# Block-sparse attention with a feed-forward network: a planner that takes VectorE and GpSimd as excluding each other instruction by instruction, and changes its order by steps of moved turns and backward passes

## The chip, the cores and the metric

The kernel runs on one core of one Trainium2 chip. The metric is the device time in microseconds (us) of one execution; the time before is the median of three runs. The engines are TensorE (PE, with its weight loads as PEld), VectorE (DVE), ScalarE (ACT), GpSimd (POOL) and SyncE (SP), which issues most of the DMAs.

## What is computed

Attention over 4 batches, 8 heads, 768 positions and 64 features a head, in blocks of 32. A block of queries sees its neighbours, the first and the last block, and three sampled blocks; the first and last block see all. What comes out, as 3072 tokens of 512 features, goes through two matrix products with a leaky maximum between them.

```python
# block = 32, n_blocks = 24, sampled_blocks [24, 3]
scores = scale * np.matmul(q, k.transpose(0, 1, 3, 2))
mask = np.abs(blk_i - blk_j) <= 1
mask = mask | (blk_i == 0) | (blk_j == 0) | (blk_i == n_blocks - 1) | (blk_j == n_blocks - 1)
for qb in range(n_blocks):
    for kb in sampled_blocks[qb]:
        mask[qb * block:(qb + 1) * block, kb * block:(kb + 1) * block] = True
scores = np.where(mask, scores, -1000000000.0)
scores = scores - np.max(scores, axis=-1, keepdims=True)
attn = np.exp(scores)
attn = attn / (np.sum(attn, axis=-1, keepdims=True) + 1e-09)
attn_out = np.matmul(attn, v).astype(np.float32)
x = attn_out.transpose(0, 2, 1, 3).reshape(B * S, H * D)      # [3072, 512]
h = x @ w_in                                                  # [512, 2048]
g = np.maximum(0.01 * h, h)
out = (g @ w_out).astype(np.float32)                          # [2048, 512]
```

## The kernel before, in words

**Numbers as pairs.** Every fp32 operand of a large product is scaled and split into a high and a low float16 part, and a product is taken as high x high, high x low and low x high. The low part comes from a subtraction on DVE or POOL.

**Tiles and items.** A tile is 64 queries of one batch with all heads; four tiles make an item of 256 tokens, and there are 12 items. The first tile of a batch, T = 0, holds the queries of the first and the last block and takes all keys. Every other tile takes 256 keys, of which the sampled ones are gathered: the keys kg by POOL copies on the chip (`gather_k`, L1273, the copies at L1295, three of one task), the values vg by an indirect DMA that POOL issues (`gather_v`, L1313, L1328) from scr, where the split values v lie in DRAM. em is a tile's row of the mask.

**One unit of attention** (a tile and a pair of heads) runs through: scores in PSUM, s<-kg,qs and s<-kg,qxs (`unit_scores`, L1357); p<-s,em,nsc on DVE with the extremum mx (`unit_ttr`, L1381); the exponential p<-p,mx on ACT; pp<-p,r on ACT, the high part; pp<-p,r,pp on DVE, the low part (`unit_split`, L1423); the transpose pt, early ones by PE and ACT (o<-eye,pp and pt<-o), later ones by DMA; av<-pt,vg on PE (`pair_av`, L1452). `tile_evac` (L1472) makes the input of the feed-forward network (FFN): avt<-av on ACT, xf<-av,avt on DVE, the high part x<-xf on ACT, the low part x<-xf,x on POOL.

**The FFN.** For each item 16 half blocks of h (`ffn_h`, L1494; 12 products of 128 x 256 each) and as many output blocks o<-W,g (`ffn_o`, L1525), with ht and g in between on ACT, DVE and POOL (`ffn_max` L1512, `ffn_act2` L1517). The first two items take the weights by quarters, as soon as each is there.

**The weights** lie in DRAM as pairs of 32-bit words. `decode` (L965) puts one piece together by one ACT and three DVE instructions (W<-W, and W<-kt,W where the raw words lie in the kt buffer). The squares W<-W on PE, which stand under s<-W in the trace, give ssw; s<-ssw,ones adds it over the partitions; DVE takes the exponent exw from it and from that the scale wi_i, wi_s (or wo_i, wo_s). `finish` (L1030) then splits: W<-W,wi_s on ACT for the high part, and for the low part DVE (W<-W,wo_s), or PE with the diagonal dg and ACT (W<-h). In the same way q gets sc_i, sc_s and qa from ssq and exq.

**The order.** Nothing is issued as it is written. Each operation is recorded as a task with its engine, an estimated duration, what it reads and writes (`Engine`, L602, which is why nearly all rows of the trace have this line). `Plan.order` (L549) then lists them: `trial` (L365) runs a model of the five engines and of the DMA rings forward, where each engine that is free takes the ready task with the lowest priority number (PE adds 400 for a change of array shape); `backward` (L503) goes through the tasks from the end and gives each its latest turn, and these turns are the next trial's priorities. 24 such passes are made, and the best is kept. Then a table of 318 steps, SHIFTS (L194), each an engine, a stretch in units of 100 ns of the model's time, and an amount, is added to the priorities, all by the starts of that one best trial, and one trial gives the order. `issue` (L569) emits it; each engine runs its queue in order.

**The model's port.** DVE and POOL share a way to the on-chip memory. In `take` (L428) a task with the mark `port` starts later by 0.6 of what the other engine's marked task has left:

```python
elif k.port:
    other = "POOL" if e == "DVE" else "DVE"
    at0 += COST["port"] * max(0.0, port[other] - at0)
    port[e] = at0 + busy
```

The functions that the diff touches, with the lines of the profile:

Of the kernel before, what the change touches and what calls it, by code (L numbers as in the profile page):

```python
# [79 lines left out]
    "passes": 24,  # L80
}
# [70 lines left out]
class Task:  # L152
# [3 lines left out]
    def __init__(self, eng, kind="", port=False):  # L156
        self.eng, self.run, self.busy, self.enter, self.kind, self.loads = eng, [], 0.0, kind, kind, []
        self.port, self.parts = port, {}
# [13 lines left out]
class Part:  # L172
# [17 lines left out]
    "port": 0.6,  # L190
# [4 lines left out]
    ("all", 382, 161, 1500), ("PE", 2050, 164, 1500), ("all", 2692, 51, -500), ("all", 308, 13, 1500),  # L195
    ("all", 326, 16, -1500), ("all", 351, 11, -1500), ("all", 2467, 105, -120), ("POOL", 2435, 1, -60),
    ("PE", 1021, 26, -900), ("all", 4744, 25, -1500), ("ACT", 5485, 132, 500), ("all", 5117, 179, -900),
    ("POOL", 2682, 33, 60), ("all", 24, 13, -250), ("PE", 1505, 151, 250), ("all", 7260, 3, -60),
    ("all", 142, 140, -500), ("all", 39, 12, 250), ("SP", 7141, 187, -250), ("all", 1837, 133, 500),
    ("POOL", 3367, 133, -500), ("all", 658, 3, 1500), ("DVE", 2456, 14, 500), ("POOL", 2148, 21, -120),  # L200
    ("DVE", 5777, 39, 1500), ("ACT", 6401, 93, 250), ("DVE", 3285, 33, 1500), ("PE", 6464, 9, 500),
    ("SP", 323, 3, -250), ("PE", 3661, 1, -1500), ("DVE", 4302, 4, 900), ("DVE", 1935, 8, 60),
    ("all", 1583, 68, 900), ("PE", 6984, 1, 60), ("PE", 6019, 8, -900), ("POOL", 1568, 31, 250),
    ("all", 6226, 9, 120), ("ACT", 4881, 11, 30), ("ACT", 1320, 77, -500), ("POOL", 4117, 101, -500),
    ("all", 3109, 18, -900), ("all", 5687, 67, 30), ("all", 4594, 11, 500), ("POOL", 3842, 107, 1500),
    ("SP", 5240, 134, 120), ("ACT", 410, 8, 900), ("all", 7070, 103, 1500), ("ACT", 1074, 34, 500),
    ("PE", 5379, 90, 120), ("POOL", 2446, 35, 500), ("PE", 3340, 6, -60), ("all", 6477, 194, 60),
    ("ACT", 293, 41, -500), ("SP", 48, 89, 250), ("PE", 6718, 1, 30), ("DVE", 6388, 17, 60),
    ("all", 438, 10, -120), ("ACT", 2931, 15, 1500), ("ACT", 3436, 10, -1500), ("SP", 3767, 84, -1500),
# [88 lines left out]
class Plan:  # L298
# [250 lines left out]
    def order(self):  # L549
# [15 lines left out]
        if VERBOSE:  # L565
            print("model", max(best[2]))
# [1422 lines left out]
```

## Time and profile before

| | us |
|---|---|
| median of 3 runs | 742.38 (739.17 to 743.46) |
| profiled execution | 740.85 |
| its span | 739.0 |
| mean granted clock of PE | 0.965 |

| engine | busy, us | share of the span |
|---|---|---|
| PE | 687.2 | 93% |
| DVE | 538.1 | 73% |
| ACT | 466.6 | 63% |
| POOL | 371.2 | 50% |

A row of the timeline has the start, the duration, engine, line, operation, what is written <- what is read, and in brackets how long the engine had been idle before it and which work ended that. The granted clock is a share of full speed: 1.00 is 2.4 GHz, 0.50 is 1.2 GHz. Matmuls of a kind are gathered in one row with their count. The FFN's first product starts at 98.22 us; the work before it is attention for the first item and the first weights.

### The profile page before, as it was taken

What the parts mean: (1) busy time and instruction counts of PE and PEld (TensorE: products, weight loads), DVE (VectorE), ACT (ScalarE), POOL (GpSimd) and SP (SyncE); (2) the same over time, 40 slices, a digit from 0 to 9 for tenths busy, and PEclk for the clock granted to TensorE, in tenths of its full rate; (3) what the DMA queues carried; (4) which work ended last, traced back from release to release, by engine and by line L of the source; (5) the groups of instructions that cost most, each with busy time, mean ns of one, the idle gap of its engine ahead of it and who ended that gap; (6) DMA issues with size and microseconds to landing.
All of it is one profiled execution on the core that took longest, in us unless ns stands there. A gap on an engine that the chain in (4) does not pass through costs nothing.

```text
span 739.0 us, 21165 instructions
## 1 busy us (share of the span) xinstructions
PE 687.2 (93%) x7880; PEld 464.5 (63%) x7880; DVE 538.1 (73%) x1544; ACT 466.6 (63%) x1111; POOL 371.2 (50%) x626
## 2 busy tenths in 40 slices
PE   2675599999999999999999999999999999999997
PEld 2353465656566667667676677666666766767664
DVE  4897998899996878777788658679786766752221
ACT  6987889966964766576667556676584655541211
POOL 1466564556425566565454647546435656632221
PEclk9766699999999999999999999999999999999999
DMA  9739699997999799999998988969995865750100
GB/s 201 257 86 266 212 279 232 227 226 141 178 182 205 151 193 200 185 181 176 196 187 160 201 175 172 198 165 201 169 173 97 173 142 93 150 127 9 44 1 29
DMA packets 261939, 122.63 MB, mean 166 GB/s; under 512 B 230220, under 2 KB 242636, under 8 KB 261836
## 3 DMA queue, kind: packets, MB, share of 16 engines
q1 hardware_dynamic: 254796, 98.20, 68.0%
q0 software_dynamic: 7040, 23.07, 12.2%
q8 instruction: 62, 1.02, 0.6%
q14 instruction: 41, 0.34, 0.2%
HBM read 65.65 MB, written 12.58 MB: 106 GB/s over the span
## 4 chain that ended last, share of the span: by engine, by line
PE 74%; DVE 6%; ACT 6%; issue 3%; DMA 3%; POOL 3%; SPq 0%; POOLq 0%; ACTq 0%; DVEq 0%
PE h L602 32%; PE o L602 31%; PE av L602 6%; PE s L602 5%; DVE W L602 2%; ACT W L602 2%; DMA vg<-scr,vrow 1%; ACT pp L602 1%; DMA pt<-pp 1%; ACT p L602 1%; DMA kt<-in_moe_w_in_dram 1%; DVE p L602 1%; DVE pp L602 1%; POOL allow L602 1%; POOL kg L1295 0%
## 5 line engine op out<-in xcount | busy, mean ns | idle before, releaser
L602 PEld LDWEIGHTS <-W 128*128 128x128 f16 (+1 forms) x2480 | 235.8, 99 | 56.1 <-DVE W L602 7.1
L602 PE MATMUL h<-x,W 128*128 128x256 f16 x2304 | 270.5, 273 | 0.2 <-POOL x L602 0.2
L602 PE MATMUL o<-W,g 128*128 128x512 f16 x1152 | 267.7, 379 | 0.7 <-DVE ob L602 0.6
L602 POOL TENSOR_TENSOR g<-ht,g 128x512 f16<-128x512 f32 x96 | 116.9, 1217 | 175.8 <-DVE g L602 145.4
L602 PEld LDWEIGHTS <-g 128*128 128x128 f16 x1152 | 109.5, 98 | 118.6 <-issue 4.9
L602 DVE SCALAR_TENSOR_TENSOR pp<-p,r,pp 128x256 f16<-128x256 f32 (+1 forms) x208 | 123.5, 612 | 26.5 <-ACT pp L602 25.8
L602 ACT ACTIVATE p<-p,mx 128x256 f32<-128x256 f32 (+1 forms) x208 | 107.1, 516 | 56.2 <-DVE mx L602 53.5
L602 ACT ACTIVATE pp<-p,r 128x256 f16<-128x256 f32 (+1 forms) x208 | 100.3, 515 | 33.3 <-DMA pt<-pp 18.2
L602 ACT ACTIVATE ht<-h,gs 128x512 f32<-128x512 f32 x80 | 54.5, 682 | 102.8 <-PE h L602 81.0
L602 DVE SCALAR_TENSOR_TENSOR ht<-h,gd,ht 128x512 f32<-128x512 f32 x80 | 59.8, 747 | 75.4 <-ACT ht L602 75.1
L1328 POOL DMA_INDIRECT vg<-scr,vrow x88 | 90.8, 1032 | 46.1 <-PE av L602 21.5
L1295 POOL COPY kg<-kt 128x128 int32 x264 | 85.4, 359 | 37.4 <-PE h L602 23.7
L602 DVE CUSTOM_DVE_ANT_0 p<-s,em,nsc 128x256 f32<-128x256 f32 x116 | 52.9, 474 | 14.3 <-PE s L602 13.3
L602 PE MATMUL av<-pt,vg 128*64 128x64 f16 (+1 forms) x2112 | 54.1, 208 | 4.9 <-DMA vg<-scr,vrow 2.5
L602 PEld LDWEIGHTS <-vg 128*64 128x64 f16 x2112 | 45.5, 114 | 19.5 <-issue 16.4
L602 POOL TENSOR_TENSOR x<-xf,x 128x256 f16<-128x256 f32 x48 | 36.1, 753 | 37.2 <-ACT x L602 30.6
L602 DVE CAST g<-ht 128x512 f16<-128x512 f32 x80 | 34.3, 429 | 9.5 <-PE o L602 7.3
L602 PEld LDWEIGHTS <-qs 128*32 128x32 f16 (+1 forms) x768 | 23.5, 98 | 26.2 <-issue 22.5
L602 ACT ACTIVATION_READ_ACCUMULATOR p<-p,mx 128x1 f32 x208 | 39.1, 188 | 0.0
L602 DVE COPY kg<-kt 128x512 f16<-128x512 f16 x96 | 33.8, 365 | 1.5 <-PE h L602 1.5
L602 PE MATMUL s<-kg,qs 128*32 128x256 f16 x464 | 31.4, 287 | 3.1 <-DVE mx L602 2.9
L602 PE MATMUL s<-kg,qxs 128*32 128x256 f16 x464 | 31.0, 283 | 0.0
(129 smaller groups left out, 801.4 us busy)
## 6 DMA issues: line engine op xcount, KB each, us to landing
v<-in_v_dram SPq DMA_DIRECT2D x32, 192.0 KB
qxs<-qs SPq DMA_DIRECT2D x48, 128.0 KB
scr<-v SPq DMA_DIRECT2D x16, 384.0 KB
vg<-scr SPq DMA_DIRECT2D x44, 128.0 KB
rq<-in_q_dram SPq DMA_DIRECT2D x20, 256.0 KB
W<-in_moe_w_in_dram SPq DMA_DIRECT2D x5, 1024.0 KB
out_dram<-ob SPq DMA_DIRECT2D x20, 256.0 KB
rk<-in_k_dram SPq DMA_DIRECT2D x24, 192.0 KB
```

The lines of the kernel that those rows point to most:

```text
L602: self.plan.task(self.eng, lambda: f(*a, **k), busy, late, reads, writes, kind, loads, port)
L1295: tc.nc.gpsimd.tensor_copy(out=kg.ap.bitcast(I32)[:, :, slot * BLOCK // 2:(slot + 1) * BLOCK // 2], in_=kt.ap.bitcast(I32)[:, :, bass.ds(o ...
L1328: tc.nc.gpsimd.indirect_dma_start(into.ap, None, scr[b].ap, bass.IndirectOffsetOnAxis(ap=at.ap, axis=0))
```

## The change

Three things change in the planner; the recorded operations are the same.

1. The model of the port. A port now holds when the other engine's marked task began to use it, a grain, and when it ends. A marked task waits for the whole rest of the other's, DVE's wait less 150 ns. For POOL's task of three copies kg<-kt the wait goes only to the end of the copy that is running (grain 330 ns).
2. SHIFTS is a new table with a fifth field. Each step adds its amount by the starts of the present best trial. With -1 nothing follows; otherwise a trial follows, and then so many backward passes, each with a trial, so that the next step sees new starts and new priorities.
3. Two settings, `xlo` and `glo`, could give the low parts of x and g of the first items to DVE. Both are 0.

```diff
-    "port": 0.6,
+    "port": 150.0,
 SHIFTS = (
-    ("all", 382, 161, 1500), ("PE", 2050, 164, 1500), ("all", 2692, 51, -500), ("all", 308, 13, 1500),
...
+    ("all", 716, 15, 500, -1), ("all", 192, 105, -60, 0), ("all", 130, 4, -30, 0), ("SP", 650, 128, 500, 0),
+    ("PE", 2232, 131, 60, -1), ("all", 1454, 144, 60, -1), ("all", 1428, 110, 250, 0),
...
-        mode, port = [""], {"DVE": 0.0, "POOL": 0.0}
+        mode, port = [""], {"DVE": (0.0, 0.0, 0.0), "POOL": (0.0, 0.0, 0.0)}
...
             elif k.port:
-                other = "POOL" if e == "DVE" else "DVE"
-                at0 += COST["port"] * max(0.0, port[other] - at0)
-                port[e] = at0 + busy
+                since, grain, until = port["POOL" if e == "DVE" else "DVE"]
+                rest = until - at0 if at0 >= since else 0.0
+                if rest > 0 and grain:
+                    rest = min(rest, grain - (at0 - since) % grain)
+                at0 += max(0.0, rest - (COST["port"] if e == "DVE" else 0.0))
+                port[e] = at0 + k.port[0], k.port[1], at0 + busy
...
-        if SHIFTS:
-            for eng, at, wide, by in SHIFTS:
-                for i, k in enumerate(self.tasks):
-                    if eng in ("all", k.eng) and at * 100.0 <= best[1][i] < (at + wide) * 100.0:
-                        prio[i] += by
+        for eng, at, wide, by, passes in SHIFTS:
+            for i, k in enumerate(self.tasks):
+                if eng in ("all", k.eng) and at * 100.0 <= best[1][i] < (at + wide) * 100.0:
+                    prio[i] += by
+            if passes < 0:
+                continue
             best = self.trial(prio, CFG["stay"])
+            for _ in range(passes):
+                prio = self.backward(best[1], best[2])
+                best = self.trial(prio, CFG["stay"])
...
             plan.task("POOL", copies, t, t, cells(kt) | cells(offs),
-                      cells(kg[:, :, at:at + NR * BLOCK]) | {("registers",)}, port=True)
+                      cells(kg[:, :, at:at + NR * BLOCK]) | {("registers",)},
+                      port=(t - CFG["kcopy"] * NR, CFG["kcopy"]))
...
-        nc.gpsimd.tensor_tensor(out=xs[:, 1], in0=xf, in1=xs[:, 0], op=ALU.subtract)
+        (nc.vector if it.n < CFG["xlo"] else nc.gpsimd).tensor_tensor(out=xs[:, 1], in0=xf, in1=xs[:, 0], op=ALU.subtract)
```

The order moves nearly everywhere. Three places follow. In the rows a name's number is that of its buffer, so av0 and s1 are PSUM banks, and W_84 is the whole weight store.

**PE, near 67 us of the trace of before.** First before, where the sum s1_64<-ssw1_180 stands behind four groups of products with vg0_88:

```order
L602 MATMUL av0_70<-pt4_155,vg0_88 64x2x32
...
L602 MATMUL av0_70<-pt3_149,vg0_88 64x128
L602 LDWEIGHTS ones_74
L602 MATMUL s1_64<-ssw1_180,ones_74 128x1
L602 LDWEIGHTS qs1_168
L602 MATMUL s1_64<-kg0_86,qs1_168 32x256
```

Then with the change:

```order
L576 MATMUL s1_64<-kg0_86,qxs1_169 32x256
L576 LDWEIGHTS ones_74
L576 MATMUL s1_64<-ssq2_170,ones_74 128x1
L576 LDWEIGHTS ones_74
L576 MATMUL s1_64<-ssw1_180,ones_74 128x1
L576 LDWEIGHTS pp3_143
L576 MATMUL o1_66<-eye16_76,pp3_143 128x128
...
L576 LDWEIGHTS vg0_88
L576 MATMUL av0_70<-pt2_148,vg0_88 64x2x32
```

The sum of squares of a weight piece has moved ahead of the first product with the gathered values, and the sum for the third half of q stands beside it.

**DVE, around the xf of the fourth tile of the first item (91.92 us in the trace of before).** Before:

```order
L602 SCALAR_TENSOR_TENSOR xf_179<-av0_70,avt_177 128x256
L602 TENSOR_SCALAR W_84<-W_84 128x1024
L602 TENSOR_SCALAR wi1_i_189<-exw2_188 128x1
L602 SCALAR_TENSOR_TENSOR W_84<-kt0_85,W_84 128x1024
L602 RECIPROCAL wi1_s_190<-wi1_i_189 128x1
L602 SCALAR_TENSOR_TENSOR W_84<-W_84 128x1024
L602 ISA p0_114,mx4_157<-s0_63,em1_165,nsc5_193 128x256
L602 ISA mx4_157 128x1
L602 ISA p1_115,mx5_159<-s1_64,em1_165,nsc5_193 128x256
L602 ISA mx5_159 128x1
L602 SCALAR_TENSOR_TENSOR xf_179<-av0_70,avt_177 128x256
L602 SCALAR_TENSOR_TENSOR W_84<-W_84 128x1024
```

With the change; the first row is that xf:

```order
L576 SCALAR_TENSOR_TENSOR xf_179<-av0_70,avt_177 128x256
L576 RECIPROCAL wi1_s_190<-wi1_i_189 128x1
L576 RECIPROCAL sc_s3_126<-sc_i3_125 128x1
L576 SCALAR_TENSOR_TENSOR W_84<-W_84,wo0_s_183 128x2x512
L576 TENSOR_SCALAR W_84<-W_84 128x1024
L576 ISA p0_114,mx4_157<-s0_63,em1_165,nsc5_193 128x256
L576 ISA mx4_157 128x1
L576 SCALAR_TENSOR_TENSOR W_84<-kt0_85,W_84 128x1024
L576 ISA p1_115,mx5_159<-s1_64,em1_165,nsc5_193 128x256
L576 ISA mx5_159 128x1
```

The two p, the scales wi_s and sc_s, one split W<-W,wo_s and one decoding step W<-kt,W stood ahead of the fourth xf and now stand behind it.

**PE, around the h block at 165.9 us of the trace of before.** Before, two score blocks stand ahead of h0_67:

```order
L602 MATMUL o1_66<-W_84,g1_211 128x512
L602 LDWEIGHTS qs0_102
L602 MATMUL s1_64<-kg0_86,qs0_102 32x256
...
L602 LDWEIGHTS qs0_102
L602 MATMUL s0_63<-kg0_86,qs0_102 32x256
...
L602 LDWEIGHTS W_84
L602 MATMUL h0_67<-x1_212,W_84 128x256
...
L602 MATMUL s0_63<-W_84 128x128
```

With the change:

```order
L576 MATMUL s1_64<-kg0_86,qxs0_103 32x256
L576 LDWEIGHTS W_84
L576 MATMUL h0_67<-x1_212,W_84 128x256
...
L576 MATMUL s0_63<-W_84 128x128
...
L576 MATMUL s1_64<-ssw3_195,ones_74 128x1
L576 LDWEIGHTS W_84
L576 MATMUL h1_68<-x1_212,W_84 128x256
...
L576 LDWEIGHTS qs0_102
L576 MATMUL s0_63<-kg0_86,qs0_102 32x256
```

The second of the two score blocks, s0_63<-kg0_86,qs0_102, has moved behind the squares of W and four half blocks of h.

## Rows read from the trace of the kernel before

**Rows 1.** The page: busy time of each engine, and the chain that ended last.

```profile
PE 687.2 (93%) x7880; PEld 464.5 (63%) x7880; DVE 538.1 (73%) x1544; ACT 466.6 (63%) x1111; POOL 371.2 (50%) x626
PE 74%; DVE 6%; ACT 6%; issue 3%; DMA 3%; POOL 3%; SPq 0%; POOLq 0%; ACTq 0%; DVEq 0%
```

**Rows 2.** Stretches: us, busy of PE, PEld, DVE, ACT, POOL, PEclk, DMA share, GB/s.

```profile
0.00:62.00 62.00, 32.80 (x365) 23.71 (x365) 46.75 (x138) 50.91 (x102) 27.42 (x71) 0.81 0.66 183
62.00:85.90 23.90, 13.63 (x178) 10.36 (x179) 19.81 (x52) 18.72 (x39) 14.40 (x23) 0.50 0.96 285
85.90:98.20 12.30, 8.47 (x106) 4.43 (x106) 11.25 (x30) 8.87 (x20) 7.14 (x12) 0.86 0.67 200
98.20:165.00 66.80, 65.47 (x695) 40.74 (x694) 61.37 (x158) 58.81 (x129) 35.96 (x56) 1.00 1.11 234
165.00:200.00 35.00, 33.90 (x379) 22.00 (x379) 32.67 (x99) 27.50 (x67) 19.40 (x35) 1.00 0.84 160
200.00:260.00 60.00, 58.87 (x689) 39.27 (x687) 48.83 (x142) 39.50 (x96) 27.47 (x49) 1.00 0.95 181
260.00:700.00 440.00, 439.56 (x5252) 302.45 (x5251) 309.58 (x921) 256.76 (x657) 231.37 (x374) 1.00 0.83 158
700.00:739.00 39.00, 34.52 (x223) 21.52 (x220) 7.82 (x14) 5.50 (x8) 8.08 (x7) 0.98 0.04 14
```

**Rows 3.** Timeline near 69 us: start, duration, engine, line, operation, idle time before.

```profile
59.37 1.32 POOL L1328 DMA_INDIRECT vg<-scr,vrow  x1 [0.30 <-issue]
...
67.09 1.82 PE L602 MATMUL av<-pt,vg 128*64 128x64 f16 x44 [2.49 <-DMA vg<-scr,vrow]
...
68.84 0.18 PE L602 MATMUL s<-ssw,ones 128*128 128x1 bf16 x1
68.95 0.38 ACT L602 ACTIVATE avt<-av 128x256 f32<-128x256 f32 x1 [2.15 <-PE av L602]
...
69.63 0.16 DVE L602 TENSOR_SCALAR exw<-s 128x1 int32<-128x1 int32 x1 [3.18 <-PE s L602]
```

**Rows 4.** Timeline of DVE, 83.9 to 92.3 us.

```profile
83.93 0.15 DVE L602 RECIPROCAL sc_s<-sc_i 128x1 f32<-128x1 f32 x1
...
84.39 1.27 DVE L602 SCALAR_TENSOR_TENSOR W<-W,wo_s 128x1024 f16<-128x1024 f32 x1
...
88.12 1.70 DVE L602 SCALAR_TENSOR_TENSOR W<-kt,W 128x1024 int32<-128x1024 int32 x1
...
91.34 0.47 DVE L602 CUSTOM_DVE_ANT_0 p<-s,em,nsc 128x256 f32<-128x256 f32 x1
...
91.92 0.42 DVE L602 SCALAR_TENSOR_TENSOR xf<-av,avt 128x256 f32<-128x256 f32 x1
92.26 1.22 DVE L602 SCALAR_TENSOR_TENSOR W<-W 128x1024 int32<-128x1024 int32 x1
```

**Rows 5.** Timeline of ACT, 84.6 to 93.3 us.

```profile
84.61 0.71 ACT L602 ACTIVATE qa<-rq,sc_s 128x512 f16<-128x512 f32 x1
...
89.93 1.15 ACT L602 ACTIVATE W<-W,wi_s 128x1024 f16<-128x1024 f32 x1 [1.94 <-DVE wi_s L602]
...
93.24 0.58 ACT L602 ACTIVATE W<-h 128x512 f16<-128x512 f32 x1
```

**Rows 6.** Timeline: the FFN's first product, and PE's wait at 165.5 us.

```profile
95.20 0.66 POOL L602 TENSOR_TENSOR x<-xf,x 128x256 f16<-128x256 f32 x1
...
98.22 1.47 PE L602 MATMUL h<-x,W 128*128 128x256 f16 x12
...
165.52 0.29 PE L602 MATMUL s<-kg,qs 128*32 128x256 f16 x4 [1.61 <-DVE mx L602]
```

**Rows 7.** Timeline at 281 us; then one group of DVE, 165 to 200 us.

```profile
280.73 2.67 DVE L602 SCALAR_TENSOR_TENSOR pp<-p,r,pp 128x256 f16<-128x256 f32 x1 [0.34 <-ACT pp L602]
281.43 0.75 POOL L1295 COPY kg<-kt 128x128 int32 x3
...
L602 DVE SCALAR_TENSOR_TENSOR pp<-p,r,pp 128x256 f16<-128x256 f32 x11 | 8.4, 760 | 0.2 <-ACT pp L602 0.2
```

More of the change, by code (lines that the diff above doesn't have):

```diff
@@ L80 @@
     "passes": 24,
+    "xlo": 0,
+    "glo": 0,
 }
@@ L200 @@
[L200 to L209, printed above, removed]
@@ new lines @@
+    ("SP", 944, 70, 900, -1), ("SP", 6232, 109, 3000, -1), ("POOL", 1093, 1, -500, 0),
+    ("all", 1328, 52, 500, -1), ("SP", 1866, 5, -900, -1), ("POOL", 4575, 186, -3000, 0),
+    ("DVE", 994, 113, 900, -1), ("all", 3191, 16, 500, 0), ("PE", 717, 5, -900, -1), ("all", 326, 32, -500, -1),
+    ("all", 6756, 190, 500, 0), ("all", 1599, 37, -60, -1), ("DVE", 4960, 24, 1500, -1),
+    ("POOL", 430, 29, -120, 0), ("POOL", 1340, 154, -500, -1), ("SP", 1885, 8, 60, -1),
+    ("ACT", 6214, 105, -60, 0), ("SP", 195, 5, 60, -1), ("all", 4628, 9, -500, 0), ("all", 91, 44, -250, 0),
@@ new lines @@
+    ("all", 930, 144, -1500, 0), ("all", 4086, 8, 900, 0), ("all", 1994, 31, -120, -1),
+    ("PE", 6386, 13, -1500, -1), ("SP", 1636, 31, 3000, 0), ("PE", 4055, 7, 900, -1),
+    ("POOL", 1824, 5, -250, -1), ("SP", 6793, 12, -30, 0), ("all", 1254, 26, 60, -1), ("ACT", 252, 3, 900, -1),
+    ("DVE", 1009, 16, -250, 0), ("all", 5292, 8, -1500, 0), ("PE", 5617, 15, -1500, -1),
+    ("ACT", 7273, 3, -900, -1), ("ACT", 5987, 22, -30, 0), ("SP", 1127, 3, 500, 0), ("all", 323, 124, 900, -1),
+    ("all", 6658, 5, 1500, 0), ("PE", 1414, 86, -250, -1), ("ACT", 5300, 116, 250, 0),
@@ new lines @@
+    ("ACT", 776, 165, 900, 0), ("all", 307, 18, 120, -1), ("all", 5165, 38, 3000, 0), ("SP", 108, 3, -60, -1),
+    ("all", 446, 7, -250, 0), ("DVE", 4136, 3, -250, -1), ("all", 591, 9, 120, 0), ("all", 144, 2, -120, 0),
+    ("SP", 1685, 23, 3000, 0), ("POOL", 325, 7, 3000, -1), ("POOL", 1357, 6, 120, -1), ("all", 968, 3, 900, 0),
+    ("DVE", 7286, 21, 250, -1), ("SP", 6796, 8, -30, -1), ("all", 1433, 152, -500, 0), ("SP", 327, 4, 1500, 0),
+    ("all", 318, 1, 250, 0), ("POOL", 1087, 2, -120, -1), ("POOL", 909, 29, -30, 0), ("SP", 781, 4, 60, -1),
@@ new lines @@
+    ("all", 5462, 29, 120, 0), ("all", 1971, 23, 1500, 0), ("all", 1432, 26, -500, 0),
+    ("POOL", 1120, 105, -30, 0), ("ACT", 492, 22, -900, 0), ("DVE", 377, 32, -3000, 0),
+    ("POOL", 1183, 174, 30, 0), ("POOL", 1032, 4, 500, -1), ("ACT", 59, 22, 900, 0), ("ACT", 228, 12, 120, -1),
+    ("all", 1315, 3, -3000, 0), ("PE", 108, 69, 3000, 0), ("PE", 88, 1, -1500, 0), ("SP", 2706, 23, 500, 0),
+    ("all", 248, 15, -1500, -1), ("PE", 181, 31, -900, -1), ("SP", 3057, 1, 3000, 0), ("PE", 424, 2, 900, -1),
@@ L270 @@
+    ("all", 5084, 2, 120, 0), ("ACT", 5170, 3, 30, 0), ("all", 6149, 34, -30, 0), ("PE", 2621, 2, 60, -1),
+    ("POOL", 1176, 25, 120, 0), ("ACT", 5662, 45, -1500, 0), ("POOL", 1506, 51, -250, -1),
[3 rows of a table added]
 )
@@ L307, in __init__, with task @@
             setattr(self, name, Engine(self, name, eng))
-    def task(self, eng, run, busy, late, reads, writes, kind="", loads=(), port=False):
+    def task(self, eng, run, busy, late, reads, writes, kind="", loads=(), port=None):
         if self.group is not None and eng == self.group.eng:
```

76 lines of the change are left out of this document (12 added, 64 removed), and 9 rows, old and new, of the table SHIFTS.

## The prediction

> **What bounds the kernel now.** I read the page's busy times first, then the chain that ended last, then busy time stage by stage, and last the timelines at the places where TensorE (PE) waits. PE is busy 93% of the span and holds 74% of the chain [rows 1]; no other engine comes near over the whole run. An average hides the stages, so the table by stretch decides [rows 2]. From 260 to 700 us PE is busy 439.56 of 440.00: nothing but less PE work, or fewer waits than 0.44, can help there, and both orders hold the same instructions. From 98.2 to 260 PE loses 1.33, 1.10 and 1.13 us in three stretches. From 700 it loses 4.48 of 39.00. What is left lies ahead of 98.2 us, where the feed-forward network (FFN) starts: PE works 32.80 of the first 62 us, then 13.63 of 23.90 at a granted clock of 0.50, then 8.47 of 12.30 at 0.86. There VectorE (DVE) is the fullest engine: 19.81 of 23.90 and 11.25 of 12.30. A start that is one us shorter there is worth one us of the run, as long as what DVE and ScalarE (ACT) put off does not hold PE up behind it. That condition is a hard one: DVE is still busy 61.37 of 66.80 and 32.67 of 35.00 in the next two stretches, so it has 5.43 and 2.33 us free [rows 2].
>
> **The port rule by itself.** It changes what the planner believes, not an instruction. No row of time belongs to it; it can act only through the order. The two new settings are 0 and move nothing. So the price is that of the new order, and I go by its places.
>
> **The stall at 69 us.** In the trace of before the gather of v into vg was issued at 59.37, and PE waited 2.49 us for it before the 44 products av<-pt,vg at 67.09 [rows 3]. Behind those on PE stands one matmul of 0.18 us, s<-ssw,ones at 68.84, the sum of squares from which a weight quarter gets its scale. DVE waited 3.18 us for it before exw<-s at 69.63, and ACT waited 2.15 us for the same 44 products before avt<-av [rows 3]. This is the dearest single stall of DVE ahead of the FFN. In the new order that matmul stands ahead of the first product with vg, with only score blocks ahead of it whose data are there. If the gather lands as late as before, PE still waits, but DVE and ACT go on with the scale, the split and the decoding of weights. What is late next is DVE's own queue of decoding. The row says 3.18 us of DVE come free, and bounds are 0 (DVE only finds another wait) and -3.2; I take **-3.2**, since DVE is at 19.81 of 23.90 there and the difference, 4.09, is little more than this one stall. ACT's own stall there lies beside it and is not counted again.
>
> **Work put off behind the start of the FFN.** The first product h<-x,W runs at 98.22; its last input is the low part of x from GpSimd (POOL) at 95.20, 0.66 us long [rows 6], which follows xf<-av,avt of the fourth tile on DVE at 91.92 [rows 4]. In the new order eight instructions that stood ahead of that xf on DVE come behind it: the first is sc_s (0.15, at 83.93), the dearest are W<-W,wo_s (1.27) and W<-kt,W (1.70), the last is the second p<-s,em,nsc (0.47, at 91.34) [rows 4]. Together they take 5.63 us; one W<-W of 1.22 comes ahead instead [rows 4], so 4.41 us less stand before it. On ACT six instructions of 4.48 us in all go the same way, the first qa<-rq,sc_s (0.71), the last W<-h (0.58), among them W<-W,wi_s, before which ACT had waited 1.94 us [rows 5]. So x of the first item can be ready up to 4.4 us earlier again. But it is work put off, not removed: counted by the instructions ahead of each product, with the trace's durations, DVE and ACT have had the same work as before by the time of the product that ran at 165.9 us. Bounds: -4.4 if all of it fits into DVE's 5.43 + 2.33 us of free time [rows 2], 0 if PE waits for it later. I take **0**, because the nearest wait is one of PE on DVE in that very stage: 1.61 us before s<-kg,qs at 165.52, released by mx [rows 6].
>
> **The wait at 165.5 us.** In the new order this score block stands behind four half blocks of h with twelve products each; at 1.47 us for twelve [rows 6] that is 5.9 us of PE work later, the squares of W between them not counted. mx gets 5.9 us more and DVE has 4.4 us more to do, so the wait should be gone: **-1.6**; bounds -1.6 and 0 (the h block in its place waits for ACT or DVE as long).
>
> **The full stretch.** From 260 us on the two orders differ by 1 to 2 us of work at most places, and hardly at all from 550 on. PE has 0.44 us of idle time to win and every pair of neighbours that is now closer can wait. No row shows such a wait behind 200 us; the nearest is that of 1.61 [rows 6]. Bounds 0 and three of them, +4.8; I take one, **+1.6**, since no place stands out and PE's queue has shown hardly any slack to lose.
>
> **The port, by a row and by a rule.** At 280.73 one pp<-p,r,pp on DVE took 2.67 us; beside it POOL ran the gathered copies kg<-kt (three in 0.75 us) and more without a pause, while the same form takes a mean of 760 ns even in the crowded stretch 165 to 200 [rows 7]. So DVE was held through several POOL instructions, about 1.9 us over the mean. The Trainium skill ("SBUF — State Buffer", section "Who interferes with whom") says that the two engines share a lock, and that the one that comes second waits until the first one's instruction is finished. The trace agrees that DVE is held, and goes beyond it: the hold lasted through a row of instructions, where by that rule it would end with one copy. By the rule the new planner's picture would be right and the sum above would stand; by the row neither planner sees the dearest case.
>
> **The sum.** -3.2 + 0 - 1.6 + 1.6 = -3.2 us. The profiled execution took 740.85 us, of which the span is 739.0 and 1.85 lie around it; it becomes 737.65. It lies 1.53 under the median of the three runs (742.38), so the median becomes **739.2**. Bounds summed: -9.2 to +4.8.
>
> **Rivals.** *Given back.* What starts earlier waits later: DVE at 61.37 of 66.80 and 32.67 of 35.00 [rows 2] sets the pace from 98 to 200 us, and the start's 3.2 us return as waits of h and s on DVE. For it: both stages are over 90% full. Against it: the stall was idle time, and removing idle time on DVE is a gain for DVE too. Then only the full stretch's change is left: 742.4, somewhere from 741 to 744.4.
>
> *All of it kept.* The 4.4 us put off fit into the free 7.76 us, no new waits: -3.2 - 4.4 - 1.6 = -9.2, 733.2. For it: PE's idle time from 98 to 200 us is 2.4 us in all [rows 2]. Against it: the wait at 165.52 itself.
>
> *The clock, on the slower side.* PE's granted clock fell to 0.50 in this kernel for a whole 23.90 us while PE was busy 13.63 of them, and in 85.9 to 98.2 it was 0.86, so 0.28 x 12.3 = 3.4 us at half [rows 2]. Those 3.4 us end just before the FFN; from 98.2 on PE is busy 98% at 1.00. The change fills the time ahead in another way, and the FFN starts on another mark. If the last stretch at half clock is as long as the one before, 23.9 instead of 3.4 us, 20.5 us of it lie under full work, and half of that is lost: up to +10.2, net +7.0, 749.4. It decides against the change from 2 x 3.2 = 6.4 us more at half clock. For it: two stretches show that a fall can last so long. Against it: the FFN's dense work came out at full clock within 3.4 us.
>
> *The port, against the planner.* With DVE deferred work running where POOL does more, holds as at 280.73 come more often between 165 and 200. Three of them cost 3 x 1.9 = 5.7, less DVE's 2.33 us free = +3.4; with the start's gain gone as well (given back), 745.8 or worse; with it kept, 742.6. The rule of the skill's page would end each hold after one copy of about 0.25 us, and this rival would then be nothing.
>
> **How the numbers follow.** Forecast (736 to 741.5) 0.50; given back 0.17; all kept 0.13; clock 0.12; port 0.08. About 0.5%, 3.7 us, is what a measurement of this kernel can tell from no change: under 738.7 lies all of "all kept" and just over half of the forecast, 0.27, so faster 0.40; over 746.1 lie the clock and half of the port and a little of "given back", 0.17; the rest, 0.43, is no change. The range goes from 732.5, just under "all kept", to 747.5: it takes in the port and the milder half of the clock rival and leaves out its full price.
>
> **What would show it.** Right: no DVE wait near 3 us on s<-ssw ahead of the FFN; first h<-x,W at 91 to 95 us; no PE wait on mx near the sixteenth h product; PE from 98 to 260 with 3 to 5 us idle. Given back: the same early start, but several PE waits on DVE or ACT between 110 and 210 us that add up to it. Clock: a granted clock under 0.9 behind the first h product. Port: pp<-p,r,pp clearly over 760 ns in 165 to 200. I would be wrong altogether if the gather of vg landed later and moved all av products, or if the first h product came no earlier than 98.

## The result: slower by 0.5%, and the profile after

The change takes 745.52 us (median; 741.19 to 750.81), the kernel before, timed beside it, 741.73. The ratio is 1.0053, 95% interval 1.0034 to 1.0072: slower by 3.9 us, by a little more than the 0.5% that can be told from no change. The predicted time was 739.2. The range on record, 732.5 to 747.5, holds the measured time, but the sign is wrong: faster had 0.40, no change 0.43, slower 0.17. A ratio compares executions timed in turns and leaves out the few that were slow, so it is not the quotient of the two medians.

The profiled execution of the change took 743.80 us with a span of 741.8. It shows 2.8 of the 3.9 us. It isn't the usual one: its mean granted clock is 0.970, and 20 of the other 21 executions have 0.956 to 0.965. First the page's busy times and its chain, then the stretches of [rows 2] from 98.2 us on (columns as there):

```profile
PE 686.7 (93%) x7880; PEld 463.7 (63%) x7880; DVE 530.0 (71%) x1544; ACT 465.0 (63%) x1111; POOL 377.5 (51%) x626
PE 78%; DVE 6%; ACT 4%; DMA 4%; issue 3%; SPq 2%; POOL 2%; POOLq 0%; ACTq 0%; DVEq 0%
```

```profile
98.20:165.00 66.80, 64.67 (x670) 39.88 (x669) 59.60 (x156) 58.34 (x128) 37.67 (x57) 1.00 1.10 223
165.00:200.00 35.00, 34.46 (x381) 22.34 (x381) 30.07 (x96) 27.50 (x69) 19.43 (x35) 1.00 0.89 158
200.00:260.00 60.00, 60.00 (x692) 39.30 (x690) 50.46 (x145) 38.12 (x95) 27.99 (x49) 1.00 0.89 178
260.00:700.00 440.00, 436.39 (x5222) 299.57 (x5220) 301.81 (x916) 255.30 (x653) 231.61 (x373) 1.00 0.87 158
```

Two things stand there. DVE is 8.1 us less busy than before (538.1) [rows 1], and the time rose: DVE got its relief, and the run did not. And from 260 to 700 us PE is idle for 3.61 us, where it was idle for 0.44 [rows 2]. From 98.2 to 260 us it is idle for 2.67, where it was 3.56. In this execution the loss lies in the long stretch in which nothing was to be won. The longest waits of PE behind the first product of the FFN:

```profile
132.48 0.29 PE L576 MATMUL s<-kg,qs 128*32 128x256 f16 x4 [1.47 <-DVE exw L576]
262.03 0.29 PE L576 MATMUL s<-kg,qs 128*32 128x256 f16 x4 [0.84 <-DVE exq L576]
452.87 2.33 PE L576 MATMUL o<-W,g 128*128 128x512 f16 x10 [0.62 <-POOL g L576]
643.38 0.29 PE L576 MATMUL s<-kg,qxs 128*32 128x256 f16 x4 [1.06 <-DMA qxs<-qs]
```

The three behind 260 us make up 2.52 of the 3.61.

Timeline of the change: the first products of the FFN on PE, and the stall of the start in its new place.

```profile
93.94 1.48 PE L576 MATMUL h<-x,W 128*128 128x256 f16 x12
97.99 1.48 PE L576 MATMUL h<-x,W 128*128 128x256 f16 x12
100.62 1.47 PE L576 MATMUL h<-x,W 128*128 128x256 f16 x12
```

```profile
55.05 1.23 POOL L1303 DMA_INDIRECT vg<-scr,vrow  x1 [4.18 <-DMA scr<-v]
56.29 0.53 POOL L576 COPY em<-mask 128x128 int32<-128x128 int32 x2
56.62 0.48 DVE L576 CUSTOM_DVE_ANT_0 p<-s,em,nsc 128x256 f32<-128x256 f32 x1 [3.08 <-POOL em L576]
57.21 0.51 ACT L576 ACTIVATE p<-p,mx 128x256 f32<-128x256 f32 x1 [3.35 <-DVE mx L576]
```

The first product came at 93.94 us where it was 98.22 [rows 6], as forecast. DVE's 3.18 us at 69 us [rows 3] are gone, and 3.08 us stand at 56.62 instead: POOL now issues a gather that waits 4.18 us for the write of scr, ahead of the copies of the mask row em, and DVE and ACT wait for em.

### The profile page after: what moved, and what is told of

It is laid out like the page before. It is cut to its first block, busy times and chain, and to the rows that moved or that the text cites. A ratio compares the mean times of both kernels' runs of the same rounds, so it can differ in the third digit from the quotient of the medians.

```text
span 741.8 us, 21188 instructions
## 1 busy us (share of the span) xinstructions
PE 686.7 (93%) x7880; PEld 463.7 (63%) x7880; DVE 530.0 (71%) x1544; ACT 465.0 (63%) x1111; POOL 377.5 (51%) x626
## 4 chain that ended last, share of the span: by engine, by line
PE 78%; DVE 6%; ACT 4%; DMA 4%; issue 3%; SPq 2%; POOL 2%; POOLq 0%; ACTq 0%; DVEq 0%
PE h L576 35%; PE o L576 31%; PE av L576 6%; PE s L576 6%; SPq L576 2%; DVE W L576 2%; DMA pt<-pp 1%; ACT W L576 1%; DMA rk<-in_k_dram 1%; DVE p L576 1%; DMA qxs<-qs 1%; DVE pp L576 1%; ACT v L576 1%; ACT p L576 1%; POOL kg L1269 1%
## 5 line engine op out<-in xcount | busy, mean ns | idle before, releaser
L576 POOL TENSOR_TENSOR g<-ht,g 128x512 f16<-128x512 f32 x96 | 115.4, 1202 | 188.0 <-DVE g L576 133.1
L576 DVE SCALAR_TENSOR_TENSOR pp<-p,r,pp 128x256 f16<-128x256 f32 (+1 forms) x208 | 116.5, 577 | 42.7 <-ACT pp L576 41.3
L1269 POOL COPY kg<-kt 128x128 int32 x264 | 89.7, 376 | 46.1 <-PE h L576 22.9
L576 DVE COPY kg<-kt 128x512 f16<-128x512 f16 x96 | 36.0, 387 | 0.1
```

The lines of the kernel that those rows point to most:

```text
L576: self.eng, lambda: f(*a, **k), busy, late, reads, writes, kind, loads, (0.0, 0.0) if port else None)
L1269: tc.nc.gpsimd.tensor_copy(out=kg.ap.bitcast(I32)[:, :, slot * BLOCK // 2:(slot + 1) * BLOCK // 2], in_=kt.ap.bitcast(I32)[:, :, bass.ds(o ...
```

## The experiments

Each ratio is to the kernel before, timed on the same chip, with its 95% interval. An order can be spliced because both kernels record the same tasks with the same numbers. After 1303, 1620 and 3160 tasks both orders have done the same set of them; in the two traces these seams lie at 226.1 and 225.1 us, 281.0 and 280.4, 563.7 and 565.2.

**Where is it lost? Head and tail.** In the edits, which are shown in short, `best` is the order of the change and `was` that of before.

```diff
-        return best[0], best
+        first = set(best[0][:1303])
+        return best[0][:1303] + [i for i in was[0] if i not in first], best
```

> The order of the change for the first 1303 tasks (to about 225 us), the order of before for the rest; at that seam both orders have done the same tasks. Theory A, the loss lies in the later stretches: in the two traces the seam is at 226.1 us before and 225.1 after, so this kernel is 1.0 us faster than before (ratio 0.998 to 1.000), and its PE waits from 226 us on are those of before (under 1.5 us in all). Theory B, the new start brings queues and buffers into a state that costs later whatever the order is: as slow as the change, ratio 1.003 to 1.007, with new PE waits behind 226 us.

Measured: 742.60 us, ratio 1.0018 [1.0002, 1.0034]. The other way round, `was` for the first 1303 tasks and `best` behind:

> The order of before for the first 1303 tasks, that of the change for the rest. Theory A: the tail alone loses what the change loses and the 1.0 us that its head gains: 3.8 to 4.8 us, ratio 1.005 to 1.0065, with PE waits from 226 us on of about 3.5 us in all, among them those on qxs near 643, g near 453 and x near 434. Theory B: ratio 0.998 to 1.002.

Measured: 744.39 us, ratio 1.0064 [1.0039, 1.0089]. The tail alone costs 4.7 us. The head alone is not 1.0 us faster, as the change's profile had it, but 1.3 slower: one profiled execution had flattered it. Theory A holds for the tail by its ratio, and its gain for the head falls; theory B falls, since the tail loses without the head. Of the waits that theory A named, near 434, 453 and 643 us, the tail's profile has none over 0.3 us. What is there are 1.22 us at 262.89 for xf and 1.68 at 265.57 for exq, so the waits of one execution need not be those of the next. The two sum to 6.0 us against 3.9 for the whole, within the intervals.

The profile of the head alone shows what that of the change does not. The first h product of the FFN runs at half clock (the row behind it as in [rows 2]):

```profile
95.79 2.74 PE L669 MATMUL h<-x,W 128*128 128x256 f16 x12
95.79:98.53 2.74, 2.74 (x18) 1.99 (x15) 2.74 (x12) 2.21 (x7) 2.35 (x7) 0.50 1.00 395
```

It is 1.27 us longer than the usual 1.47 [rows 6]. In the profiles of the eight kernels here that begin with the order of the change, spliced, mended or with added work, this group of twelve took 1.61 to 2.74 us; in the change's own it took 1.48, and in all nine that begin with the order of before 1.47. So the clock is a candidate for the 1.3 us that the head loses. No experiment below changes the clock at that place, and what it costs there beside what half clock cost ahead of it in the kernel before is not shown.

**Which part of the tail?** The order of before with the change's order for one piece.

```diff
-        return best[0], best
+        head, upto = set(was[0][:1303]), set(best[0][:1620])
+        return (was[0][:1303] + [i for i in best[0][:1620] if i not in head]
+                + [i for i in was[0] if i not in upto and i not in head]), best
```

> The kernel before, with the change's order for tasks 1304 to 1620 alone (226 to 281 us); at both seams the two orders have done the same tasks. The tail as a whole cost 4.7 us (ratio 1.0064). Theory G, a single place in this piece costs most: in the run with the tail alone PE waited 1.22 and 1.68 us near 263 and 266: +2 to 3 us, ratio 1.003 to 1.004. Theory H, the loss is spread over the whole tail, by its number of tasks 0.6 us here: ratio 0.999 to 1.002.

Measured: 744.85 us, ratio 1.0029 [1.0005, 1.0053]. And with 1620 and 3160 for 1303 and 1620:

> The kernel before, with the change's order for tasks 1621 to 3160 alone (281 to 564 us). Theory H, spread: 1540 of the tail's 1857 tasks that stand in another order (behind 3160 hardly any do), so most of the 4.7 us: +3 to 4 us, ratio 1.004 to 1.0055. Theory G: +1 to 2 us, ratio 1.001 to 1.003.

Measured: 745.71 us, ratio 1.0031 [1.0002, 1.0059]. 55 us of the order cost as much as the next 283: theory G for the first piece; the second lies between the two theories. Its timeline, DVE and PE near 264 us, then the stretch by granted clock (the second last three figures of the row are PEclk, DMA share, GB/s):

```profile
261.39 0.16 PE L669 MATMUL s<-ssq,ones 128*128 128x1 bf16 x1
261.83 0.48 DVE L669 SCALAR_TENSOR_TENSOR pp<-p,r,pp 128x256 f16<-128x256 f32 x1 [1.46 <-DMA pt<-pp]
263.72 0.48 DVE L669 SCALAR_TENSOR_TENSOR pp<-p,r,pp 128x256 f16<-128x256 f32 x1 [1.41 <-ACT pp L669]
264.19 0.15 DVE L669 TENSOR_SCALAR exq<-s 128x1 int32<-128x1 int32 x1
264.39 0.38 PE L669 MATMUL s<-kg,qs 128*32 128x256 f16 x4 [1.90 <-DVE exq L669]
265.77 2.50 PE L669 MATMUL h<-x,W 128*128 128x256 f16 x12
```

```profile
264.00:268.00 4.00, 3.61 (x36) 2.51 (x36) 4.00 (x17) 3.59 (x9) 2.96 (x7) 0.57 0.98 200
```

The sum of squares s<-ssq,ones was there at 261.55. Its reader exq, 0.15 us of work, stands on DVE behind two pp<-p,r,pp, of which one waited for a transpose (DMA pt<-pp) and one for ACT, so it ran at 264.19. A score block on PE waited for exq for 1.90 us. Then the clock fell: granted 0.57 over the next 4 us, and twelve h products took 2.50 us for the usual 1.47 [rows 6]. In this execution the wait was paid nearly twice. That is not the rule: the same wait was 0.84 us in the change, 1.68 in the tail alone and 0.63 in a run further down (em first), and in none of the three did the clock fall behind it. The other piece shows a fall in its profile, behind another wait:

```profile
571.52 0.61 PE L669 MATMUL o<-W,g 128*128 128x512 f16 x2 [2.04 <-DVE g L669]
572.84 4.45 PE L669 MATMUL o<-W,g 128*128 128x512 f16 x10 [0.71 <-POOL g L669]
```

```profile
571.50:578.30 6.80, 6.07 (x36) 2.25 (x40) 1.58 (x3) 0.69 (x1) 2.30 (x2) 0.54 0.00 0
```

That wait lies just behind the piece, in the order of before. Its two waits are 2.75 us, and PE's 6.07 us of work at 0.54 lose another 2.8 (an estimate from these rows). That is more than the 2.3 us that the piece costs on the mean, so it can't stand in every execution. What the second piece costs has not been traced to a place.

**Is it that one place?** DVE's order at 261 us, the edit on the piece and on the whole change:

```diff
 xf<-av,avt
-pp<-p,r,pp
-pp<-p,r,pp
 exk<-s
 exq<-s
+pp<-p,r,pp
+pp<-p,r,pp
 sc_i<-exk
```

> The kernel before with the change's order from 226 to 281 us (which alone took 1.0029 of before), and in it one edit on DVE: exk<-s and exq<-s stand ahead of the two pp<-p,r,pp that wait for ACT, not behind them. In the profile of that piece PE waited 1.90 us at 264.39 for exq, and its granted clock was 0.50 in the rows from 264 to 267.6 right behind, where twelve products h<-x,W took 2.50 us for 1.47. Theory I, this one wait with the fall of the clock is what the piece costs: the wait goes, ratio 0.9985 to 1.001. Theory H, the cost is spread over the piece: ratio 1.002 to 1.004 again.

> The change with the same edit on DVE at 261 us (exk, exq ahead of two pp). Theory I: 1.5 to 2.5 us under the change, ratio to before 1.002 to 1.0035, no PE wait for exq near 262. Theory H: 0 to 0.8 us under it, ratio 1.004 to 1.006.

Measured: the piece 740.61 us, ratio 0.9992 [0.9966, 1.0018]; the change 741.68 us, ratio 1.0004 [0.9979, 1.0029]. Two instructions of 0.15 us, put ahead of two others, take 2.7 us off the piece and 3.6 off the change. The difference of the two ratios is 0.0037 with an uncertainty of 0.0035 for the piece, and 0.0049 with 0.0031 for the whole (the root of the squares of the two half intervals, here and below). A third pair stands further down: the change with em first took 1.0038, and with this edit as well 0.9987, a difference of 0.0051 with 0.0032. So the two instructions cost time in all three orders, and theory I holds for the piece. For the change it named 1.5 to 2.5 us and a ratio from 1.002; the gain is larger, 3.6 us with an interval from 1.3 to 5.9, and the 0.84 us of waiting in the change's own profile do not account for it. Where the rest comes from is open. DVE in the mended piece, and the same stretch by clock:

```profile
259.99 0.16 DVE L696 TENSOR_SCALAR exk<-s 128x1 int32<-128x1 int32 x1 [1.14 <-PE s L696]
260.07 0.15 DVE L696 TENSOR_SCALAR exq<-s 128x1 int32<-128x1 int32 x1
260.13 0.87 DVE L696 SCALAR_TENSOR_TENSOR pp<-p,r,pp 128x256 f16<-128x256 f32 x2
```

```profile
264.00:268.00 4.00, 4.00 (x67) 2.68 (x66) 3.94 (x13) 2.59 (x9) 2.20 (x3) 1.00 0.82 91
```

In the profiled execution of the mended change PE is idle for 0.33 us from 98.2 to 260 and 0.30 from 260 to 700:

```profile
98.20:165.00 66.80, 66.54 (x701) 42.13 (x699) 62.04 (x159) 58.77 (x130) 39.70 (x58) 1.00 1.05 220
165.00:260.00 95.00, 94.93 (x1112) 61.79 (x1111) 81.53 (x249) 67.66 (x166) 48.91 (x92) 1.00 0.88 177
260.00:700.00 440.00, 439.70 (x5209) 302.21 (x5208) 304.89 (x909) 253.55 (x650) 233.72 (x366) 1.00 0.82 156
```

That execution took 735.86 us, the best of the kernel's own, so it shows what the order can do, not what it usually does. And the edit is not what made it so: the sum s<-ssq,ones, which stands ahead of the edit, ran at 256.55 us there and at 260.10 in the profiled execution of the change.

**Why the planner did not see it.** The score block writes columns 0 to 255 of the PSUM bank s1; the sums that exk and exq read lie in columns from 384 on, by the kernel's own division of the bank. The planner's tasks depend on one another by small pieces of a tile (`cells`, here 16 columns), and in its list of what that score block waits for, exq is missing, in both kernels. In the trace the block waits for it. So the wait follows the bank and the order in which things are issued, and no model of the planner holds it. The Trainium skill states such a rule ("PSUM — Partial Sum Buffer", section "PSUM bank collisions raise a hardware error"): two engines must not touch one bank within the same group of 32 partitions at a time, whatever the columns, so accesses are to be guarded by bank and not by address. The trace fits with it: 1.90 us for a reader of other columns. What two such accesses at once would do, no run here shows.

**The start: the wait for em.**

```diff
 # GpSimd
-vg<-scr,vrow
 em<-mask
 em<-mask
+vg<-scr,vrow
 vg<-scr,vrow
```

> The change, with one edit: GpSimd makes the two copies of the mask row em before it issues the first indirect gather of v (which waits 4.18 us for the write of scr), not behind it. In the trace of the change DVE waits 3.08 us at 56.62 for em, ACT 3.35 and PE 1.71 behind it. Theory C, the start is held by that one wait: first h product 2 to 2.5 us earlier than 93.9, time 2 to 3 us under the change (ratio to before 1.001 to 1.003). Theory D, what the start gains is given back by 200 us because DVE and ACT are full there: the wait goes, the loss of PE at 226 us is the same within 0.5 us, ratio 1.004 to 1.007.

> The first 1303 tasks in the order of the change, the rest in the order of before, and em ahead of the first gather. Theories A and C together: 1.0 us from the head and 2 to 2.5 from em, 738.5 to 739.5 where before is 742, ratio 0.995 to 0.997. A and D: 741, ratio 0.998 to 1.000.

Measured: 743.71 us, ratio 1.0038 [1.0013, 1.0063], and with the tail of before 741.25 us, ratio 1.0008 [0.9983, 1.0034]. Beside their sisters (1.0053 and 1.0018) they are 1.1 and 0.7 us faster, which the intervals do not resolve. The first lies between the two theories; the second is over both, since both counted on 1.0 us from the head. In the first one DVE's wait for em went from 3.08 to a wait of 1.71 us for the scores, and its first h product came at 94.47, not earlier than 93.94: not 2 to 2.5 us earlier, which was theory C.

**The start: the sum ahead of the products with vg**, alone, in the order of before on PE:

```diff
+s1_64<-ssw1_180,ones_74
 av0_70<-pt4_155,vg0_88 and the three groups behind it
-s1_64<-ssw1_180,ones_74
 s1_64<-kg0_86,qs1_168
```

> The kernel before with one edit on PE: the sum s<-ssw,ones stands ahead of the two groups of products with vg that wait for the gather, as it does in the change; nothing else moves. The step on record says the 3.18 us that DVE waited come free and the time falls by up to 3.2 us (ratio 0.996). The rival, given back: the wait near 69 us goes or falls under 1 us, the first h product comes 0 to 1 us earlier, and the time stays, ratio 0.9985 to 1.0015.

Measured: 738.96 us, ratio 0.9975 [0.9952, 0.9997], between the step on record (0.996) and the rival (from 0.9985), and DVE still waits:

```profile
65.21 0.16 PE L694 MATMUL s<-ssw,ones 128*128 128x1 bf16 x1 [0.45 <-DVE ssw L694]
68.13 0.43 PE L694 MATMUL s<-kg,qxs 128*32 128x256 f16 x4
68.61 0.16 DVE L694 TENSOR_SCALAR exw<-s 128x1 int32<-128x1 int32 x1 [1.77 <-PE s L694]
```

The sum ended at 65.37; exw started at 68.61, which is 0.05 us after the end of the score block at 68.56. That block writes s1 too and stood between the sum and exw in the order. It is the same wait with the parts exchanged. In [rows 3] the releaser was named "PE s", and I had read it as the sum. There too a score block stands behind the sum:

```profile
69.15 0.43 PE L602 MATMUL s<-kg,qxs 128*32 128x256 f16 x4
```

The sum ended at 69.02, this block at 69.58, and exw started at 69.63. So the reader was issued ahead of the block as well:

```diff
 # DVE
+exw1_181<-s1_64
 wi0_s_174<-wi0_i_173
 kg1_87<-kt1_96
-exw1_181<-s1_64
```

> The kernel before with the sum s<-ssw,ones ahead of the products with vg, and exw<-s, its reader on DVE, issued right behind it, ahead of the score block into the same PSUM bank. Theory J, the wait near 69 us was for that score block, since it was issued between the sum and its reader: exw starts at 65 to 67 us and the DVE wait near 68.6 is under 0.5 us; time as with the sum moved alone (0.9975) or up to 1.5 us less. Theory K, the wait is for the sum or for the gather itself: DVE waits 1.5 us or more at the same place, whatever follows.

Measured: 740.65 us, ratio 1.0015 [0.9996, 1.0034]. Theory J holds for the wait, not for the time, which it put at 0.9975 or less:

```profile
66.59 0.15 DVE L694 TENSOR_SCALAR exw<-s 128x1 int32<-128x1 int32 x1
67.09 1.82 PE L694 MATMUL av<-pt,vg 128*64 128x64 f16 x44 [1.38 <-DMA vg<-scr,vrow]
70.40 2.51 DVE L694 SCALAR_TENSOR_TENSOR W<-W,wi_s 128x1024 f16<-128x1024 f32 x2 [1.95 <-ACT W L694]
```

The stall is gone and the time is no better: DVE runs ahead and then waits 1.95 us for ACT, which stands behind avt and so behind the products with vg. In this trace the gather sets this place, not the sum. In the run with 0.9975 PE waited for the gather until 66.19, here until 67.09; whether the better ratio of the two is more than chance is open.

**The wait at 165.5 us**, alone, on PE, in the order of before:

```diff
-s0_63<-kg0_86,qs0_102 and qxs0_103
 h0_67<-x1_212,W_84
 s0_63<-W_84
 h0_67<-x1_212,W_84
+s0_63<-kg0_86,qs0_102 and qxs0_103
```

> The kernel before with one edit on PE: the score block that waited 1.61 us at 165.52 stands behind the next two half blocks of h and the squares of W (3.9 us later); the other engines keep their order. The step on record says -1.6 us (ratio 0.998). The rival: the wait moves to the h block or to the next score block, ratio 0.9995 to 1.001.

Measured: 740.15 us, ratio 0.9999 [0.9974, 1.0024]. The rival holds; the wait has changed its name and kept its length. The block moved by two half blocks of h here and by four in the change.

```profile
165.25 1.36 PE L694 MATMUL h<-x,W 128*128 128x256 f16 x11 [1.62 <-POOL x L694]
```

In the change itself PE waits 0.25 us at this place, and 1.47 us at 132.48 instead.

**The clock of the start.** Added matmuls that nobody reads, at the places where PE stood still:

```diff
             for i in order:
+                for _ in range(FILL.get(i, 0)):
+                    self.nc.tensor.matmul(spare, eye16, eye16, start=True, stop=True)
                 for run in self.tasks[i].run:
                     run()
```

> The kernel before, with 223 added matmuls of 128x128 on PE whose output nobody reads, spread over the 17 places between 10 and 88 us where PE stood still, about 60% of each gap at full clock. Nothing else differs. Theory E, the half clock of the start costs: over 30 runs of before the mean granted clock answers to 48.0 us at half, and within the kernels timed so far a us more at half goes with 0.13 us more time; if the added work keeps the clock up, half clock falls under 20 us and the time by 3 to 4 us, ratio 0.994 to 0.997. Theory F, DVE and ACT set the pace there and the clock is worth nothing: the granted clock rises and the time stays, ratio 0.998 to 1.002, or it grows by the added work in PE's queue.

> The change, with 303 such added matmuls at the 19 places between 10 and 88 us where its own PE stood still. The runs of kernels with the start of the change had 54 to 59 us at half clock, those with the start of before 48 to 50. Theory E: the clock is what the new start pays for, half clock falls under 20 us and the time by 4 us or more, to 741 or less (ratio to before under 1.000). Theory F: the same as the change, ratio 1.003 to 1.007.

Measured: 743.40 us, ratio 1.0007 [0.9984, 1.0029], and 741.38 us, ratio 0.9989 [0.997, 1.0008]. The stretch from 10 to 98 us in the kernel before, in it with the added work, in the change, and in the change with the added work:

```profile
10.00:98.00 88.00, 54.29 (x646) 38.11 (x647) 75.87 (x209) 73.93 (x150) 47.43 (x92) 0.71 0.72 215
```

```profile
10.00:98.00 88.00, 63.28 (x878) 48.46 (x879) 76.87 (x213) 74.88 (x154) 47.26 (x92) 0.84 0.77 225
```

```profile
10.00:98.00 88.00, 53.40 (x673) 38.21 (x674) 78.17 (x214) 75.48 (x154) 50.01 (x92) 0.75 0.74 224
```

```profile
10.00:98.00 88.00, 62.28 (x939) 46.99 (x938) 77.89 (x210) 74.47 (x152) 50.41 (x92) 0.88 0.73 225
```

The clock rose from 0.71 to 0.84 in the kernel before, and nothing came of it: theory F there. The change gained 4.7 us, which is the number of theory E (under 1.000). In the profiled executions the gain does not lie in the start: the first h product came at 95.23, later than 93.94, and the sum s<-ssq,ones at 260.25, where it was 260.10; from 260 to 700 us PE is idle for 1.85 us, where it was 3.61, and there is no wait for exq near 262. Perhaps ACT and the transposes stood in another relation at 261 us; that was not tried, and a share of the clock is not excluded. Nor did the added work, which ends at 88 us, keep the clock up into the FFN: the first h product took 2.41 us.

**Rule or table?** The two planners with their 24 passes and no table of moved turns:

```diff
-        for eng, at, wide, by, passes in SHIFTS:
+        for eng, at, wide, by, passes in ():
```

> The planner before (port rule 0.6) with its 24 passes and no table of moved turns at all. Theory L, the table carries the order's quality: 1 to 3% slower than before, ratio 1.01 to 1.03.

> The planner of the change (ports that exclude each other) with its 24 passes and no table. Theory L: the rule by itself moves the time by less than 0.5% against the old rule without a table, either way. Theory M, the rule itself is what loses or gains: a difference of over 1% between the two kernels without a table.

Measured: 742.39 us, ratio 1.0041 [1.0019, 1.0062], with the old rule; 742.60 us, ratio 1.0051 [1.0025, 1.0077], with the new one. The rule by itself makes a difference of 0.0010 with an uncertainty of 0.0034, as theory L had it; theory M falls. It does what it is for, in one profiled execution of each: the mean of pp<-p,r,pp on DVE is 600 ns with the old rule and 566 with the new one, in the same group of the page.

```profile
L667 DVE SCALAR_TENSOR_TENSOR pp<-p,r,pp 128x256 f16<-128x256 f32 (+1 forms) x208 | 120.3, 600 | 27.6 <-ACT pp L667 27.2
```

```profile
L667 DVE SCALAR_TENSOR_TENSOR pp<-p,r,pp 128x256 f16<-128x256 f32 (+1 forms) x208 | 114.0, 566 | 29.9 <-ACT pp L667 29.1
```

The old table was worth 0.4%, not the 1 to 3% that theory L put on it. The new table with its passes has no worth that could be measured (1.0053 with it, 1.0051 without, uncertainty 0.0032). So the change lost what the old table had.

**Both mended places together, and one more.** em first and exq first in the change:

> The change with both edits: exk and exq ahead of two pp on DVE at 261 us, and em ahead of the first indirect gather on GpSimd at 56 us. If the two effects add (3.6 us and 1.1 us in the runs with one of them), ratio to before 0.998 to 1.000. If the start's gain is given back by 226 us, 1.000 to 1.0015.

Measured: 738.91 us, ratio 0.9987 [0.9967, 1.0007], in the range for two effects that add. Then also exw ahead of pp<-p,r,pp and W<-kt,W on DVE at 132 us, a second place of the same kind; and that with the order of before from 281 us on.

```diff
 # DVE
 ht<-h,ht
+exw1_181<-s1_64
 pp<-p,r,pp
 W_84<-kt,W_84
-exw1_181<-s1_64
```

> The change with three edits: exk and exq ahead of two pp on DVE at 261 us, em ahead of the first gather on GpSimd, and exw ahead of pp<-p,r,pp and W<-kt,W on DVE at 132 us, where PE waited 1.47 us for it. Theory I, each such place costs its wait: 1.0 to 1.5 us under the kernel with two edits (0.9987), ratio 0.9965 to 0.9975. Rival, given back between 132 and 200 us where DVE is full: 0.998 to 0.9995.

> The same three edits, with the change's order for the first 1620 tasks (to 281 us) and the order of before for the rest. If the change's order from 281 on costs 2.3 us as the piece alone did, ratio 0.9935 to 0.9955; if that cost was a matter of how the piece follows on what is ahead of it, the same as its sister kernel within 0.15%.

Measured: 739.26 us, ratio 0.9985 [0.9956, 1.0014], and 738.02 us, ratio 0.9963 [0.9938, 0.9987]. The place at 132 us gave nothing that shows: the first ratio lies in the rival's range, but its interval takes in theory I as well. No PE wait for exw is left there in the two profiles; there was none in that of the change with exq first alone either, which lacks this edit, so one profile does not tell what it did. The last kernel is faster than before by more than its interval, 2.7 us. That the tail of before is better than the mended tail of the change (0.0022) is not resolved (0.0038).

## Why the prediction was wrong

The sum was -3.2 us and the measured difference +3.9. Two terms failed, and neither alone turned the sign. What the text had for the start and its first stages, up to 226 us, was -3.2 - 1.6; the head alone measured +1.3, which is 6.1 us off. What it had for the rest was +1.6; the tail alone measured +4.7, which is 3.1 off. With the head as forecast, the tail's 4.7 would have left the time where it was.

**The full stretch, +1.6 with bounds 0 and 4.8: too small.** Measured for the tail alone: +4.7, near the upper end. I had priced new waits by one row of 1.61 us and taken one, since "no place stands out". One did. Two things were missing. The first is that a reader of a sum and a score block in the same bank hold each other up, by the order of issue; in [rows 3] such a case stood under a name that I read otherwise. Put right, that one place gave back 3.6 of the 3.9 us (1.3 to 5.9). The second is that a wait of 1.9 us on PE can cost nearly twice its length by the clock, as one execution shows (2.50 us for 1.47). I had the clock as a rival at the start of the FFN alone.

**The stall at 69 us, -3.2: wrong, and with the wait at 165.5 us the larger miss.** The wait went, as forecast, but it came back as 3.08 us at 56.62 for em, behind a gather that now stands ahead of it on POOL. The text on record did not follow POOL's queue, past which that step had been moved. And the term alone, tried without the rest of the change, gave 0.9975 with less of the stall left and 1.0015 with none: what ends last there is the gather, by way of avt on ACT. That explains why the 3.2 us did not come; what makes the head 1.3 us slower than before is open, with em (about 1 us, not resolved) and the clock at the first h product as candidates.

**Work put off, 0: the right number by another way.** The first h product came 4.3 us earlier (94 us lies within the 91 to 95 that were named), the third 2.0 us earlier, and by 124 us little of it was left: both kernels have then done eight groups of h products and twelve products o<-W,g. The text expected PE to wait for DVE or ACT. It did not wait at all; first before, then with the change:

```profile
98.22:123.78 25.56, 25.56 (x262) 16.66 (x261) 23.83 (x59) 23.16 (x47) 14.22 (x22) 1.00 1.05 254
93.94:123.80 29.86, 29.86 (x303) 19.52 (x300) 29.39 (x78) 28.07 (x59) 18.41 (x28) 1.00 1.05 231
```

PE was busy all the time at full clock, with 4.3 us more of its own other work behind the first product: nine groups of h<-W,dg where there had been seven, and three of the squares s<-W where there had been one. Most of it had stood ahead of that product; what is left of the lead is one group of squares, about 0.9 us. The text counted what DVE and ACT put off, and not what PE did.

**The wait at 165.5 us, -1.6: wrong.** Alone it gave 0.9999, with another wait of 1.62 us in its place, which the bound of 0 had said. In the change it went, and PE waits 1.47 us for exw at 132.48.

**The port: neither rival nor forecast.** DVE was held less, not more: it was 8.1 us less busy, and pp<-p,r,pp took a mean of 502 ns from 165 to 200 us, where the rival's sign was clearly over 760 [rows 7]. The time did not follow, with PE as the bound.

**What would show it.** Of the signs on record for "given back", the early start was seen, with one PE wait of 1.47 us on DVE between 110 and 210 us and not several. (Its price stood at 742.4; with only the full stretch's +1.6 left it would have been 744.0.) PE's idle time from 98 to 260 us was 2.67 us, under the 3 to 5 that were named. The sign for the clock, under 0.9 behind the first h product, is not in the change's profile but in those of its relatives: at the first product itself (0.50 in the head alone), at 264 and 571 us in the two pieces, and 0.65 at 387 us in the kernel before with the added matmuls.

## What to carry to other kernels

Where an engine is busy 99% over hundreds of microseconds, a new order has little to win and every new neighbourhood to lose. An earlier start of the bound engine's main work is no gain if that engine was full and only its own other work moved behind it: count it too. Look first for short instructions that a busy engine waits for and that stand on another queue behind a long wait. A planner that tracks memory by address does not see waits that come from a shared bank; either it learns of the bank, or such readers get a bank of their own. A profile of one execution with 2 us of scatter between executions does not price a term of 1 us, and its waits may be missing from the next execution; see whether its mean clock is a usual one, splice the orders and time the parts.

## What the runs showed of the hardware

A single wait of 1.90 us in an otherwise full stretch was followed by granted 0.57 over 4 us, one of 2.04 and 0.71 by 0.54 over 6.8 us. Waits of 1.61 and 1.62 us at 165 us were not followed by a fall in the rows, nor were 1.22 and 1.68 us near 265 in the tail alone. A score block in columns 0 to 255 of a bank waited for the reader of a sum in the same bank's columns from 384 on, and such a reader for a score block; both waits went when the order of issue changed. A raised clock in a start where DVE and ACT set the pace (0.84 for 0.71) gave nothing.
